# One pool of PSUM banks for the MLP and the segments, additions by VectorE in the last quarter, and memory rows turned earlier

## The chip, the core and the metric

The kernel runs on one core of a Trainium2 chip. The core has TensorE (matrix products, which it writes into PSUM), VectorE and ScalarE (elementwise work, both can read and write PSUM), GpSimd (POOL in the profile) and a queue engine, SP. DMA transfers between the DRAM and the on-chip memory SBUF are issued from SP, ScalarE or POOL, in each one's program order, and all of them run on the same 16 DMA engines. PSUM has eight banks; a bank holds 128 x 512 numbers of 32 bits, the result of one matmul of 512 columns. The metric is the device time of one execution in microseconds, as the median of several.

## The reference

The input x has 2048 tokens of 1024 numbers. It is normalized to xn, and two branches are added to it:

```python
x + A_ref(layernorm(x), mem0, Wq, Wk, Wv, Wo, 32) + B_ref(layernorm(x), w1, b1, w2, b2)

# B: an MLP over all tokens
h = gelu(xn @ w1 + b1)            # 2048 x 3584
return h @ w2 + b2                # 2048 x 1024

# A: 64 segments of 32 tokens, one after the other
mem = mem0                        # 8 rows of 1024
for s in range(64):
    h = concat([mem, xn[32*s : 32*s+32]])
    q, k, v = h @ Wq, h @ Wk, h @ Wv      # 32 heads of 128
    o = softmax(mask(q @ k.T / sqrt(128))) @ v
    o = o @ Wo
    mem = o[:8]                   # the next segment needs this
    outs.append(o[8:])
```

The segments depend on each other through the eight memory rows, while the MLP is free of such a chain. Data are bfloat16, sums are 32 bits.

## The kernel before

The work has two stages. First comes the MLP, in four quarters of 512 tokens. Then come the 64 segments. The code writes out the order of instructions by hand; each engine executes its own list in that order and waits on semaphores for the others.

A quarter of the MLP has 28 blocks of *first products* (`first_product`, L498): block fb takes 8 matmuls into one PSUM bank. ScalarE adds the bias (L572), VectorE and ScalarE compute GELU in several steps, and `gelu_tail` (L560, L561) writes the result, one of 28 blocks, into tiles called gT. Then come the *second products* of the quarter: for each of four groups of 128 tokens (t) and each half of the 1024 output columns (nb), 28 matmuls (fc = 0 to 27) are summed in one bank. In the first three quarters one bank after the other is completed (L619), VectorE adds the bias b2 (kept as the broadcast tile `b2bc`) and x, and the row is stored to the DRAM tensor `R_n` by `keep_R` (L448). `turn_R` (L485, L487) copies these rows into the layout in which the segments read them.

The last quarter (tg = 3) is different, because the memory of w1, w2 and gT is handed over to the weights of the segments while it runs. Of 64 weight units of 0.5 MB that a segment uses, 47 stay resident in SBUF (`fetch_resident`, L247 and L249) and 17 are streamed through six slots (`start_stream`, L279), two of these from copies kept in PSUM. A unit can be fetched as soon as the tile at its place has been read for the last time. During the last first products, every second block frees a tile of w1. Then, in the kernel before:

- `put_mem` (L315, L321, L325) turns the eight rows of mem0 with small matmuls against an identity into a bank of its own; VectorE copies them to `hr_home`, the operand of segment 0. After it, half of a unit of Wo is loaded over the source of these rows, into `d_oL` (L640).
- Eight banks are taken, six from the rotation of the first products (`ps`) and two from those used for transposes (`pT`); t = 3 has the latter two.
- For fc = 0 to 19 (`FC - TAIL`, TAIL = 8), each fc goes to all eight banks (L647), and `freed(fc)` then fetches the units that take the places of w2 and gT.
- For t = 3, the bias b2 and x are added by four matmuls: ones times the row b2 (L667) and identity times x (L669).
- For t = 0, 1, 2 the last eight fc are done one t after the other, and VectorE adds b2bc (L677) and x (L678).
- For t = 3 the last eight fc follow for each half; at the second half, `freed(20)` to `freed(27)` are called. The halves are copied out by ScalarE (L686), VectorE (L687) and ScalarE (L688), and `keep_R` issues the store from ScalarE's queue.

Only then does the pool of PSUM banks for the MLP end, and that of the segments begin: three banks that rotate as accumulators (`acc`), one for scores and other small things (`mixed`), and four that hold copies of weights (`kept`). Segment 0 begins with VectorE copying the preloaded halves of Wo from `d_oL` and `kq` into `kept` (L268), and TensorE starts the products for K (L791, from `half_pass`). They need the resident and streamed K units, `hr_home` with the memory rows, and a bank `acc`. In each segment the passes K, Q, K, Q, V, V of eight units each are followed by 16 units of Wo (L1049), and by `put_mem` for the next segment. Segment 0 also does the products for the last rows of four segments (`hrL`), and its pace of `unit_done` starts the following streams, seven late resident units and, in the following segments, the last rows of `turn_R` on POOL's queue.

The functions that the change touches, with their lines:

Of the kernel before, what the change touches and what calls it, by code (L numbers as in the profile page):

```python
# [10 lines left out]
BF16 = mybir.dt.bfloat16  # L11
# [6 lines left out]
P = 128  # L18
# [30 lines left out]
SCRATCH = 320  # L49
SMALL = 3776  # L50
LEAD = 6
TAIL = 8
EARLY_SEGS = 7
LEAD_FIRST = 4
SCORES_0 = (6, 6, 6, 5)
# [60 lines left out]
def kernel(  # L116
# [212 lines left out]


    NT = S // P
    with tc.tile_pool(name="ma", bufs=2) as ma, tc.tile_pool(name="mps", bufs=6, space=PSUM) as mps:
        eps_t = ma.tile([P, 1], F32, name="eps_t", bufs=1)
        nc.vector.memset(eps_t[:], EPS)
        ones = ma.tile([1, P], BF16, name="ones", bufs=1)
# [72 lines left out]
            return xn  # L408

        def turned(xn):  # L410
            pT = mps.tile([P, KT, P], BF16, name="pT", bufs=2)
            for kt in range(KT):
                nc.tensor.transpose(pT[:, kt, :], xn[:, kt * P:(kt + 1) * P], ident)
            return pT
# [88 lines left out]
                    stop=(kt == KT - 1),  # L503
                )

        def new_ps():
            return mps.tile([P, 512], F32, name="ps")

        idle = new_ps()
        for _ in range(WARM):  # L510
            nc.tensor.matmul(
# [24 lines left out]
        keep_xT(0, xnT)  # L536

        b1col = ma.tile([P, FC], F32, name="b1col", bufs=1)
        pst = mps.tile([P, KT, P], BF16, name="pT", bufs=2)
# [5 lines left out]
        for tg in range(4):  # L545
# [18 lines left out]
            for fb in range(FC):  # L564
                if tg == 0 and fb < len(begun):
                    ps = begun[fb]
                    first_product(ps, fb, xnT, 8, 16)
                else:
                    ps = new_ps()
                    first_product(ps, fb, xnT, 0, 16)  # L570
                xb = ma.tile([P, 512], BF16, name="g_xb", bufs=3)
                nc.scalar.activation(  # L572
                    out=xb[:, :], in_=ps[:, :], func=ACT.Identity, bias=b1col[:, fb:fb + 1], scale=1.0
                )
                u = ma.tile([P, 512], BF16, name="g_u")
                nc.vector.tensor_tensor(out=u[:, :], in0=xb[:, :], in1=xb[:, :], op=ALU.mult)
                nc.vector.tensor_scalar(
                    out=u[:, :], in0=u[:, :], scalar1=0.044715, scalar2=1.0, op0=ALU.mult, op1=ALU.add
                )
                nc.vector.tensor_tensor(out=u[:, :], in0=u[:, :], in1=xb[:, :], op=ALU.mult)  # L580
                if pend is not None:
                    gelu_tail(*pend)
                pend = (fb, u, xb)
                if last and fb % 2:
                    place = f"w1_{fb // 2}"
                    if place in RING:
                        start_stream(place)
                    else:
                        fetch_resident(place)
            gelu_tail(*pend)  # L590

            if tg == 0:
                for nb in range(2):
                    cs = slice(nb * 512, nb * 512 + 512)
                    ps = mps.tile([P, 512], F32, name="ps")
                    nc.tensor.matmul(ps[:, :], lhsT=ones[0:1, :], rhs=b2row[0:1, cs], start=True, stop=True)
                    nc.scalar.copy(out=b2bc[:, cs], in_=ps[:, :])

            if not last:
# [11 lines left out]
                for t in range(4):  # L611
                    ttg = 4 * tg + t
                    xn = ln_apply(ttg + 4)
                    rsb = xtoks[ttg]
                    for nb in range(2):
                        cs = slice(nb * 512, (nb + 1) * 512)
                        ps = mps.tile([P, 512], F32, name="ps")
# [12 lines left out]
                    keep_R(ttg, rsb)  # L630
# [3 lines left out]
            else:  # L634
# [6 lines left out]
                pss = [mps.tile([P, 512], F32, name="ps") for _ in range(6)]  # L641
                pss += [mps.tile([P, 512], F32, name="pT", bufs=2) for _ in range(2)]
                halves_of = [slice(512 * nb, 512 * nb + 512) for nb in range(2)]
                x = xtoks[4 * tg + 3]

                def second_product(fc, t, nb, stop):
                    nc.tensor.matmul(  # L647
                        pss[2 * t + nb][:, :],
                        lhsT=gts[fc // 4][:, fc % 4, t * P:(t + 1) * P],
                        rhs=w2_sb[fc // 2][:, fc % 2, halves_of[nb]],  # L650
                        start=(fc == 0),
                        stop=stop,
                    )

                def freed(fc):
                    if fc % 2:
                        fetch_resident(f"w2_{fc // 2}")
                    if fc % 4 == 3:
                        fetch_resident(f"gT{fc // 4}")

                for fc in range(FC - TAIL):
                    for t in range(4):
                        for nb in range(2):
                            second_product(fc, t, nb, False)
                    freed(fc)
                for nb, cs in enumerate(halves_of):
                    nc.tensor.matmul(pss[6 + nb][:, :], lhsT=ones[0:1, :], rhs=b2row[0:1, cs], start=False, stop=False)  # L667
                for nb, cs in enumerate(halves_of):
                    nc.tensor.matmul(pss[6 + nb][:, :], lhsT=ident, rhs=x[:, cs], start=False, stop=False)  # L669
                for t in range(3):  # L670
                    for fc in range(FC - TAIL, FC):
                        for nb in range(2):
                            second_product(fc, t, nb, fc == FC - 1)
                    r = xtoks[4 * tg + t]
                    for nb, cs in enumerate(halves_of):
                        ps = pss[2 * t + nb]
                        nc.vector.tensor_tensor(out=ps[:, :], in0=ps[:, :], in1=b2bc[:, cs], op=ALU.add)  # L677
                        nc.vector.tensor_tensor(out=r[:, cs], in0=ps[:, :], in1=r[:, cs], op=ALU.add)  # L678
                    keep_R(4 * tg + t, r)
                for nb in range(2):  # L680
                    for fc in range(FC - TAIL, FC):
                        second_product(fc, 3, nb, fc == FC - 1)
                        if nb:
                            freed(fc)
                    if nb == 0:
                        nc.scalar.copy(out=x[:, 0:512], in_=pss[6][:, :])  # L686
                nc.vector.tensor_copy(out=x[:, 512:768], in_=pss[7][:, 0:256])  # L687
                nc.scalar.copy(out=x[:, 768:1024], in_=pss[7][:, 256:512])  # L688
                keep_R(4 * tg + 3, x)

    with tc.tile_pool(name="late", bufs=1) as late, \
            tc.tile_pool(name="banks", bufs=1, space=PSUM) as banks:
# [15 lines left out]
        def let_go(ps):  # L713
            free_banks.append(bank_of.pop(id(ps))[0])

        mixed = banks.tile([P, 512], F32, name="mixed")
# [5 lines left out]
        masks_at = there[:, 32 * NL:32 * NL + NX + GRP * 16]  # L722
        mask_order = masks_at[:, 0:NX]
        mask_left = masks_at[:, NX:].rearrange("p (g q) -> p g q", g=GRP)
        kept = banks.tile([P, 4, 512], F32, name="kept")

        def keep(unit, c0, w, bank):

            copy_bits(kept[:, bank, :].bitcast(U32), w.bitcast(U32))
            kept_in.setdefault(unit, []).append((c0, kept[:, bank, :]))  # L730

        place_in_stream = {}

# [544 lines left out]
```

## Time and profile before

| | us |
|---|---|
| timed runs | 1809.34, 1813.58, 1815.01 |
| median | 1813.58 |
| profiled execution, its own time | 1810.81 |
| its span, first to last instruction | 1809.0 |
| first products of the last quarter begin | 311.7 |
| second products of the last quarter begin | 360.3 |
| segment 0 begins | 414.7 |
| memory rows for segment 1 (L315) | 452.5 |
| memory rows for segment 2 | 475.8 |
| TensorE busy, of the span | 1702.7 (94%) |
| VectorE / ScalarE / GpSimd busy | 983.8 / 686.6 / 300.5 |

Times within the span count from its first instruction. In the profile's rows, PE is TensorE, PEld its loading of the stationary operand, DVE is VectorE, ACT ScalarE; SPq and ACTq are issues of DMA transfers from these queues. "L791" is line 791 of the kernel. A row of the list of waits reads "who waits <- for whom: us in total, times, longest". In the table by stretches each row has the stretch, its length, the busy time of TensorE, its loads, VectorE, ScalarE and GpSimd with the number of instructions, the granted TensorE clock as a share of full speed, the share of the DMA engines' time in use, and GB/s. In the chain, each row is a start, a duration and the work that held the end at that point.

### The profile page before, as it was taken

Reading aid. Unit: us, or ns where it says so; the run is one execution under the profiler, and the core shown is the slowest. Engines: PE = TensorE matmul, PEld = TensorE weight load, DVE = VectorE, ACT = ScalarE, POOL = GpSimd, SP = SyncE. Lnnn points to the kernel's source line nnn. Section 1 sums busy time; section 2 is a strip of 40 time slices with the busy share of each in tenths; the row PEclk is TensorE's granted clock in tenths of the full one; section 3 lists DMA queues with packets and bytes.
Section 4 is the critical chain, followed back from the end, with each engine's and each line's share of the span. In section 5 each row is a group of like instructions: output and inputs, shape, how many; then the busy total and the mean of one; then the engine's idle time right before and its main releaser. Section 6 shows DMA issues by size and latency. Waiting matters only on the chain.

```text
span 1809.0 us, 71476 instructions
## 1 busy us (share of the span) xinstructions
PE 1702.7 (94%) x31161; PEld 894.6 (49%) x31161; DVE 983.8 (54%) x2517; ACT 686.6 (38%) x1698; POOL 300.5 (17%) x586
## 2 busy tenths in 40 slices
PE   8999999997999999999999999999999999999998
PEld 4444444444445555555554555554545555555544
DVE  7657483805555555555555555555555555555544
ACT  6334260702333333333333334343433334334333
POOL 0000000411132111111111212111111211111111
PEclk9999999999999999999999999999999999999999
DMA  9931111769999999999999999999999999999998
GB/s 289 310 100 48 53 48 37 247 221 339 370 385 389 376 385 374 386 374 379 387 380 380 385 396 388 384 389 364 382 384 375 387 369 393 380 375 392 384 390 315
DMA packets 221310, 592.07 MB, mean 327 GB/s; under 512 B 46195, under 2 KB 76515, under 8 KB 220996
## 3 DMA queue, kind: packets, MB, share of 16 engines
q1 hardware_dynamic: 197584, 567.08, 83.7%
q0 software_dynamic: 16896, 16.85, 2.9%
q8 instruction: 244, 4.00, 0.9%
q10 hardware_dynamic: 6516, 3.57, 0.7%
q14 instruction: 70, 0.57, 0.1%
HBM read 573.43 MB, written 28.90 MB: 333 GB/s over the span
## 4 chain that ended last, share of the span: by engine, by line
PE 78%; DMA 11%; DVE 4%; ACT 4%; issue 3%; ACTq 0%; DVEq 0%; POOL 0%; POOLq 0%
PE acc L791 38%; PE acc L1049 12%; PE ps L498 11%; PE ps L619 8%; DMA u<-Wc_O 7%; DMA u<-Wc_V 3%; PE ps L647 2%; ACT mixed L960 2%; PE acc L1000 1%; PE mixed L908 1%; DVE kq L875 1%; DVE pd_main L973 1%; ACT kq L870 1%; PE pT L647 1%; PE mixed L914 1%
## 5 line engine op out<-in xcount | busy, mean ns | idle before, releaser
L791 PE MATMUL acc<-u,hr_home 128*32 128x512 bf16 x11520 | 760.2, 380 | 16.7 <-issue 7.3
L791 PEld LDWEIGHTS <-hr_home 128*32 128x32 bf16 x12288 | 351.0, 96 | 286.0 <-issue 39.1
L791 PE MATMUL acc<-u,hrL 128*32 128x512 bf16 x2880 | 256.4, 380 | 6.4 <-issue 3.8
L498 PE MATMUL ps<-u 128*128 128x512 bf16 (+1 forms) x920 | 194.4, 374 | 2.0 <-ACT u L418 2.0
L268 DVE TENSOR_SCALAR u<-kept 128x512 uint32<-128x512 uint32 x254 | 163.2, 684 | 57.9 <-PE acc L791 43.4
L843 ACT CAST d_oL<-acc 128x512 bf16<-128x512 f32 x143 | 82.0, 584 | 263.3 <-PE acc L791 254.8
L619 PE MATMUL ps<-u 128*128 128x512 bf16 x672 | 147.0, 379 | 0.0
L1049 PE MATMUL acc<-u,d_oL 128*32 128x512 bf16 x1944 | 132.7, 381 | 9.7 <-issue 6.0
L498 PEld LDWEIGHTS <-u 128*128 128x128 bf16 x920 | 89.8, 98 | 104.9 <-issue 2.4
L1049 PEld LDWEIGHTS <-kq 128*32 128x32 bf16 x3908 | 102.7, 96 | 76.5 <-ACT kq L1019 21.8
L973 DVE TENSOR_TENSOR pd_main<-kq,mixed 128x320 bf16<-128x320 bf16 x128 | 62.5, 488 | 133.1 <-ACT mixed L960 133.1
L875 DVE STREAM_TRANSPOSE kq<-kq 128x512 bf16<-128x512 bf16 x128 | 91.1, 711 | 73.5 <-ACT kq L870 71.1
L870 ACT CAST kq<-acc 128x512 bf16<-128x512 f32 (+2 forms) x192 | 85.3, 444 | 114.5 <-PE acc L791 84.8
L1049 PE MATMUL acc<-u,kq 128*32 128x256 bf16 (+1 forms) x2372 | 116.0, 313 | 13.6 <-DMA u<-Wc_O 11.4
L1240 POOL DMA_DIRECT2D out_dram<-hr_home x168 | 85.2, 514 | 221.5 <-DVE hr_home L1207 221.1
L847 ACT CAST kq<-acc 128x512 bf16<-128x512 f32 x128 | 75.1, 587 | 111.6 <-PE mixed L914 105.5
L791 PEld LDWEIGHTS <-hrL 128*32 128x32 bf16 x3072 | 88.1, 96 | 59.0 <-issue 6.0
L938 DVE TENSOR_TENSOR kq<-kq,mixed 128x96 bf16<-128x96 bf16 (+1 forms) x256 | 38.1, 190 | 125.5 <-ACT kq L928 68.6
L619 PEld LDWEIGHTS <-u 128*128 128x128 bf16 x672 | 65.3, 98 | 77.4 <-DVE g_u L580 0.4
L1049 PEld LDWEIGHTS <-d_oL 128*32 128x32 bf16 x2592 | 65.3, 96 | 66.1 <-issue 20.0
L572 ACT ACTIVATE g_xb<-ps,b1col 128x512 bf16<-128x512 f32 x112 | 76.8, 686 | 55.5 <-PE ps L498 54.7
L960 ACT ACTIVATE mixed<-mixed,small_consts 128x160 f32<-128x160 f32 x256 | 94.2, 368 | 8.4
(133 smaller groups left out, 2010.4 us busy)
## 6 DMA issues: line engine op xcount, KB each, us to landing
u<-Wc_K SPq DMA_DIRECT2D x256, 512.0 KB
u<-Wc_V SPq DMA_DIRECT2D x256, 512.0 KB
u<-Wc_O SPq DMA_DIRECT2D x256, 512.0 KB
u<-Wc_Q SPq DMA_DIRECT2D x192, 512.0 KB
u<-in_B_w_dram SPq DMA_DIRECT2D x28, 512.0 KB
u<-in_A_Wq_dram SPq DMA_DIRECT2D x13, 512.0 KB
u<-in_A_Wv_dram SPq DMA_DIRECT2D x12, 512.0 KB
u<-in_A_Wk_dram SPq DMA_DIRECT2D x9, 512.0 KB
```

The lines of the kernel that those rows point to most:

```text
L268: nc.vector.tensor_single_scalar(out=out, in_=in_, scalar=0, op=ALU.bitwise_or)
L498: nc.tensor.matmul(ps[:, SEG * s0:SEG * s1].rearrange("p (s t) -> p s t", t=SEG), lhsT=w1_sb[fb // 2][:, kt, (fb % 2) * P:(fb % 2 + 1) * P ...
L572: nc.scalar.activation(out=xb[:, :], in_=ps[:, :], func=ACT.Identity, bias=b1col[:, fb:fb + 1], scale=1.0)
L619: nc.tensor.matmul(ps[:, :], lhsT=gts[fc // 4][:, fc % 4, t * P:(t + 1) * P], rhs=w2_sb[fc // 2][:, fc % 2, cs], start=(fc == 0), stop=(fc ...
L791: nc.tensor.matmul(o, lhsT=lhs[:, i, :], rhs=m, start=(i == seq[0]), stop=(i == seq[-1]), tile_position=(0, 32 * j),)
L843: cp(out=out, in_=ps.rearrange("p (h e) -> p h e", e=32))
L870: nc.scalar.copy(out=q_home[:, h0:h1, NL:40], in_=ps[:, 32 * h0:32 * h1].rearrange("p (h e) -> p h e", e=32))
L875: nc.vector.transpose(out=home, in_=home)
L960: nc.scalar.activation(out=mixed[:, 160 * b:160 * b + 160], in_=mixed[:, 0:160], func=ACT.Exp, scale=-1.0, bias=off[:, b:b + 1],)
L973: nc.vector.tensor_tensor(out=pdA.rearrange("p c b q -> p b c q"), in0=prA[:, None, :, :].to_broadcast([P, 2, 4, 40]), in1=dd, op=ALU.mult,)
L1049: nc.tensor.matmul(acc[r0:r0 + rows, 0:256 * len(blocks)], lhsT=lhsT, skip_group_check=True, rhs=o_columns(t, k, blocks), start=start, sto ...
L1240: loads.dma_start(out=out_flat[rows, 256 * j:256 * j + 256], in_=res[32 * j:32 * j + NX, :])
```

## The change

One pool of eight PSUM banks, with one tag per bank, now serves both stages. `new_ps` hands out banks 0 to 5 in turn for the products, 6 and 7 for transposes. The accumulators of the segments get the banks of the last quarter's t = 0 and the first half of t = 1, `mixed` the second half of t = 1, and `kept` (now four tiles instead of one) those of t = 2 and t = 3. So each user of a bank waits for the bank's last user alone.

`put_mem` and the load into `d_oL` move to block 20 of the last quarter's first products; `put_mem` takes one bank from the rotation there.

In the second products of the last quarter, t = 0 runs two steps (AHEAD) ahead of the others, and all eight banks go through all 28 fc without a separate tail. The four matmuls for b2 and x are gone. Instead VectorE adds b2bc and x into each bank in the middle of its sum: bank n after fc = 3 + 2n. The matmul of that bank for the next fc is left out at its step, and made up one step later, just before the regular one. A unit is fetched when all eight banks have used the tile at its place. At the end the banks are only copied out: t = 0 by VectorE and ScalarE when it is complete, 12 matmuls before the last; then t = 1 and t = 2 by both, and t = 3 by ScalarE alone.

```diff
-TAIL = 8
+AHEAD = 2
+ADD_FIRST = 4
+ADD_STEP = 2
+MEM_AT = 20
...
+    banks = ctx.enter_context(tc.tile_pool(name="banks", bufs=1, space=PSUM))
+    turns = {"ps": deque(range(6)), "pT": deque((6, 7))}
+    def new_ps(way="ps"):
+        k = turns[way][0]
+        turns[way].rotate(-1)
+        shape, kind = ([P, 512], F32) if way == "ps" else ([P, KT, P], BF16)
+        ps = banks.tile(shape, kind, name=way, tag=f"bank{k}")
+        place_of[id(ps)] = k, ps
+        return ps
...
+                if last and fb == MEM_AT:
+                    put_mem(o_sb, nxt["hT"], new_ps(), wide=False)
+                    nc.sync.dma_start(out=d_oL[:, 0:DM], in_=Wo_v[:, h + 1, :])
...
-                put_mem(o_sb, nxt["hT"], mps.tile([P, 512], F32, name="ps"), wide=False)
-                nc.sync.dma_start(out=d_oL[:, 0:DM], in_=Wo_v[:, h + 1, :])
...
+                    taken[fc] += 1
+                    if taken[fc] == 8:
+                        if fc % 2:
+                            fetch_resident(f"w2_{fc // 2}")
+                        if fc % 4 == 3:
+                            fetch_resident(f"gT{fc // 4}")
+
+                def row_out(t, engines):
+                    x = xtoks[4 * tg + t]
+                    for nb, cp in enumerate(engines):
+                        cp(out=x[:, 512 * nb:512 * nb + 512], in_=pss[2 * t + nb][:, :])
+                    keep_R(4 * tg + t, x)
...
-                for nb, cs in enumerate(halves_of):
-                    nc.tensor.matmul(pss[6 + nb][:, :], lhsT=ones[0:1, :], rhs=b2row[0:1, cs], start=False, stop=False)
-                for nb, cs in enumerate(halves_of):
-                    nc.tensor.matmul(pss[6 + nb][:, :], lhsT=ident, rhs=x[:, cs], start=False, stop=False)
...
+                add_at = {ADD_FIRST + ADD_STEP * n: n for n in range(8)}
+                for step in range(FC + AHEAD):
                     for t in range(4):
+                        fc = step if t == 0 else step - AHEAD
+                        if not 0 <= fc < FC:
+                            continue
                         for nb in range(2):
...
+                            n = 2 * t + nb
+                            if add_at.get(fc) == n:
+                                continue
+                            if add_at.get(fc - 1) == n:
+                                second_product(fc - 1, t, nb)
+                            second_product(fc, t, nb)
+                            if add_at.get(fc + 1) == n:
+                                ps, cs = pss[n], slice(512 * nb, 512 * nb + 512)
+                                for r in (b2bc, xtoks[4 * tg + t]):
+                                    nc.vector.tensor_tensor(out=ps[:, :], in0=ps[:, :], in1=r[:, cs], op=ALU.add)
+                    if step == FC - 1:
+                        row_out(0, (nc.vector.tensor_copy, nc.scalar.copy))
+                for t, engines in ((1, (nc.scalar.copy, nc.vector.tensor_copy)), (2, (nc.scalar.copy, nc.vector.tensor_copy)), (3, (nc.scalar.copy, nc.scalar.copy))):
+                    row_out(t, engines)
...
-        free_banks = deque(f"acc{k}" for k in range(3))
+        free_banks = deque(f"bank{k}" for k in seg_banks[:3])
...
-        kept = banks.tile([P, 4, 512], F32, name="kept")
+        kept = [banks.tile([P, 512], F32, name="kept", tag=f"bank{k}") for k in seg_banks[4:]]
```

More of the change, by code (lines that the diff above doesn't have):

```diff
@@ L331 @@
     NT = S // P
-    with tc.tile_pool(name="ma", bufs=2) as ma, tc.tile_pool(name="mps", bufs=6, space=PSUM) as mps:
+    banks = ctx.enter_context(tc.tile_pool(name="banks", bufs=1, space=PSUM))
+    turns = {"ps": deque(range(6)), "pT": deque((6, 7))}
+    place_of = {}
+    def new_ps(way="ps"):
[5 more added lines that the diff above has]
+        return ps
+    with tc.tile_pool(name="ma", bufs=2) as ma:
         eps_t = ma.tile([P, 1], F32, name="eps_t", bufs=1)
@@ L410, in turned @@
         def turned(xn):
-            pT = mps.tile([P, KT, P], BF16, name="pT", bufs=2)
+            pT = new_ps("pT")
             for kt in range(KT):
@@ L504, in first_product @@
                 )
-        def new_ps():
-            return mps.tile([P, 512], F32, name="ps")
         idle = new_ps()
@@ L538 @@
         b1col = ma.tile([P, FC], F32, name="b1col", bufs=1)
-        pst = mps.tile([P, KT, P], BF16, name="pT", bufs=2)
+        pst = new_ps("pT")
         pst_flat = pst.rearrange("p a b -> p (a b)")
@@ L594 @@
                     cs = slice(nb * 512, nb * 512 + 512)
-                    ps = mps.tile([P, 512], F32, name="ps")
+                    ps = new_ps()
                     nc.tensor.matmul(ps[:, :], lhsT=ones[0:1, :], rhs=b2row[0:1, cs], start=True, stop=True)
@@ L616 @@
                         cs = slice(nb * 512, (nb + 1) * 512)
-                        ps = mps.tile([P, 512], F32, name="ps")
+                        ps = new_ps()
                         for fc in range(FC):
@@ L638, with second_product @@
                 start_stream("xn3")
-                put_mem(o_sb, nxt["hT"], mps.tile([P, 512], F32, name="ps"), wide=False)
-                nc.sync.dma_start(out=d_oL[:, 0:DM], in_=Wo_v[:, h + 1, :])
[L641 to L646, printed above, removed]
+                pss = [new_ps() for _ in range(6)]
+                pss += [banks.tile([P, 512], F32, name="ps", tag=f"bank{k}") for k in turns["pT"]]
+                seg_banks = [place_of[id(ps)][0] for ps in pss[:6]] + list(turns["pT"])
+                taken = [0] * FC
+                def second_product(fc, t, nb):
                     nc.tensor.matmul(
@@ L649, in second_product @@
                         lhsT=gts[fc // 4][:, fc % 4, t * P:(t + 1) * P],
-                        rhs=w2_sb[fc // 2][:, fc % 2, halves_of[nb]],
+                        rhs=w2_sb[fc // 2][:, fc % 2, nb * 512:nb * 512 + 512],
                         start=(fc == 0),
-                        stop=stop,
-                    )
[L655 to L659, printed above, removed]
@@ L661 @@
-                for fc in range(FC - TAIL):
+                        stop=(fc == FC - 1),
+                        skip_group_check=True,
+                    )
+                    taken[fc] += 1
[9 more added lines that the diff above has]
+                    keep_R(4 * tg + t, x)
@@ L668 @@
-                for nb, cs in enumerate(halves_of):
[L669 to L689, printed above, removed]
@@ L696 @@
-    with tc.tile_pool(name="late", bufs=1) as late, \
-            tc.tile_pool(name="banks", bufs=1, space=PSUM) as banks:
+                            n = 2 * t + nb
[8 more added lines that the diff above has]
+                                    nc.vector.tensor_tensor(out=ps[:, :], in0=ps[:, :], in1=r[:, cs], op=ALU.add)
@@ L698 @@
+                    if step == FC - 1:
+                        row_out(0, (nc.vector.tensor_copy, nc.scalar.copy))
+                for t, engines in ((1, (nc.scalar.copy, nc.vector.tensor_copy)), (2, (nc.scalar.copy, nc.vector.tensor_copy)), (3, (nc.scalar.copy, nc.scalar.copy))):
+                    row_out(t, engines)
+    with tc.tile_pool(name="late", bufs=1) as late:
         nc.scalar.preload_act_table_set("natural_log_exp_and_others")
         small = deque()
-        free_banks = deque(f"acc{k}" for k in range(3))
+        free_banks = deque(f"bank{k}" for k in seg_banks[:3])
@@ L714, in let_go @@
             free_banks.append(bank_of.pop(id(ps))[0])
-        mixed = banks.tile([P, 512], F32, name="mixed")
+        mixed = banks.tile([P, 512], F32, name="mixed", tag=f"bank{seg_banks[3]}")
         trs = [
@@ L724 @@
         mask_left = masks_at[:, NX:].rearrange("p (g q) -> p g q", g=GRP)
-        kept = banks.tile([P, 4, 512], F32, name="kept")
+        kept = [banks.tile([P, 512], F32, name="kept", tag=f"bank{k}") for k in seg_banks[4:]]
         def keep(unit, c0, w, bank):
-            copy_bits(kept[:, bank, :].bitcast(U32), w.bitcast(U32))
-            kept_in.setdefault(unit, []).append((c0, kept[:, bank, :]))
+            copy_bits(kept[bank].bitcast(U32), w.bitcast(U32))
+            kept_in.setdefault(unit, []).append((c0, kept[bank]))
         place_in_stream = {}
```

2 lines of the change are left out of this document (removed).

## The prediction, made before the run

> **What bounds the kernel now.** I read five views, from the whole to the place of the edit. The first is the page: shares of the chain that ended last, and the row of DMA traffic over 40 slices of 45.2 us.
>
> ```profile
> PE 78%; DMA 11%; DVE 4%; ACT 4%; issue 3%; ACTq 0%; DVEq 0%; POOL 0%; POOLq 0%
> GB/s 289 310 100 48 53 48 37 247 221 339 370 385 389 376 385 374 386 374 379 387 380 380 385 396 388 384 389 364 382 384 375 387 369 393 380 375 392 384 390 315
> ```
>
> TensorE carries 78% of the chain. The weights stream at about 385 GB/s from slice 10 on, but only 221 and 339 GB/s pass in slices 8 and 9 (362 to 452 us), where the last quarter of the MLP meets segment 0. All edits lie between the first products of that quarter (from 311.7 us) and segment 0. The second view is the chain in order of time there.
>
> ```profile
> 363.32 0.23 DVE hr_home L325
> 363.60 0.38 PE ps L647
> 363.97 0.43 PE pT L647 x2
> 364.40 2.33 PE ps L647 x6
> 366.73 0.85 PE pT L647 x2
> 367.59 1.52 PE ps L647 x6
> 369.11 0.43 PE pT L647 x2
> ...
> 398.90 0.53 PE pT L667 x2
> 399.43 0.54 PE pT L669 x2
> 399.97 10.36 PE ps L647 x48
> 410.33 3.47 PE pT L647 x16
> 413.82 0.43 DVE u L687
> 414.28 0.38 ACT u L688
> 414.70 5.17 PE acc L791 x92
> 419.87 11.12 DMA u<-Wc_Q
> ```
>
> The chain leaves TensorE at three points: for VectorE's copy of the memory rows (L325), for the copies that end the MLP (L687, L688), and in segment 0 for weights. Matmuls of 512 columns come every 0.216 us (48 in 10.36 us). The third view is TensorE's list of waits from 360 to 480 us: total, times, longest.
>
> ```profile
> PE acc L791 <- DMA u<-Wc_Q: 2.8, 2, 1.7
> PE ps L647 <- DVE hr_home L325: 2.0, 1, 2.0
> PE acc L791 <- DMA u<-Wc_V: 1.8, 4, 0.9
> PE acc L1049 <- DMA u<-Wc_O: 1.7, 3, 0.7
> PE acc L791 <- ACT u L688: 0.9, 1, 0.9
> PE acc L791 <- DMA hrL<-rowsL_d: 0.8, 1, 0.8
> ```
>
> The fourth is the table by stretches: after the 2.0 us wait the granted clock (third column from the right) was 0.63 and 0.52 for two stretches of 2 us; and from 404 to 406 us the DMA engines moved nothing.
>
> ```profile
> 364.00:366.00 2.00, 2.00 (x7) 0.75 (x6) 0.00 (x0) 0.00 (x0) 0.00 (x0) 0.63 0.80 215
> 366.00:368.00 2.00, 2.00 (x6) 0.76 (x5) 0.00 (x0) 0.00 (x0) 1.05 (x2) 0.52 0.94 375
> 404.00:406.00 2.00, 2.00 (x11) 0.88 (x10) 1.96 (x3) 0.00 (x0) 0.00 (x0) 1.00 0.00 0
> ```
>
> The fifth, the instructions on the tile ps, prices the additions (ns: least, median, most).
>
> ```profile
> L677 DVE TENSOR_TENSOR ps<-ps,b2bc x6: 689/694/700, 403.2 to 411.5; 128x512 f32<-128x512 f32 x6
> L678 DVE TENSOR_TENSOR u<-ps,u x6: 691/692/692, 404.0 to 412.2; 128x512 bf16<-128x512 f32 x6
> ```
>
> **The change, part by part.**
>
> *Memory rows amid the first products (put_mem at block 20).* The eight small matmuls (0.23 us together at 360.15) and VectorE's copy (0.22 us) are moved, not removed. What goes is the wait: the sixth bank of the second products was put_mem's own, and its copy stood behind the last GELU steps in VectorE's queue, until 363.6. In the new place the bank is asked for again six blocks later, 6 x 8 x 0.216 = 10.4 us, and the copy is queued behind two to three GELU steps of 0.4 us. Gain: 2.03 us.
>
> The half clock goes with it: the 17 matmuls from 363.60 to 369.11 took 5.51 us against 17 x 0.216 = 3.67. Gain: 1.84, say 1.85 us. What shows that the wait caused it: idles of 1.68 us (before 428.4) and 1.77 us (before 435.0) left the clock at 1.00 in this trace, that of 2.03 did not. Ends: 0 (it was not the wait) and 1.85; I take 1.85.
>
> [...]
>
> The copy of Wo's half into d_oL moves ahead of four w1 fetches, xn2 and xn3 on SP's queue. It waits only for put_mem's matmuls, and the fetch behind it for the next block anyway. Cost 0; without that cover one block, 1.7 us, on a queue with idle DMA engines behind it.
>
> *Bias and x by VectorE.* Four matmuls go (L667, L669): 0.53 + 0.54 = 1.07 us. There come 16 additions in place of 12; each pair takes 1.43 us (403.24 to 404.67). A bank's matmul is left out at one step and made up at the next, so between two uses of it lie 14 other matmuls, 3.0 us, less 0.2 us of the last one's tail: 2.8 us of cover for 1.43 us plus a handover. VectorE is idle there otherwise (the stretches from 364 on show 0.00). The tightest is the first, behind the last GELU product, which ends at 363.4; bank 0 is left at about 363.3 and wanted at about 366.1. Cost 0; if the cover went, 8 x 1.43 = 11.4 us.
>
> *Row 0 two steps ahead, banks handed on one by one.* Segment 0's first product takes the bank of row 0, emptied some 18 matmuls (3.9 us) before the end; before, it waited 413.80 to 414.70 for L687 and L688. Gain 0.90 us. The banks at the start of the second products have slack too: row 0 goes alone for two steps, and the bank of block 27 is wanted nine matmuls (1.9 us) on, its reading by ScalarE over after 0.7.
>
> ScalarE now holds four of the last six evacuations and three stores behind the last matmuls: copies 0.59, a store's issue 0.33 (rows 413.39 and 414.68), then the table load 1.28. Counted through, its last copy ends 2.4 us and the table load 4.0 us after the last matmul; before, the table load ended 1.6 us after segment 0's start. The first K evacuation queued behind it ends at about 4.8 us, before at 3.4 (417.52 + 0.58 - 414.70); its bank is wanted by the second accumulator of Q at 4.3 (419.01). VectorE's keep copies wait for row 3 and come 1 to 1.5 us later too; the scores that need them start 10 us in. Cost 0.5 us, ends 0 and 1.4.
>
> *Weights earlier.* Before, six fetches of 0.52 MB (w2_10 to w2_13, gT5, gT6) were all released by the last eight matmuls: at segment 0's start 3.15 MB were outstanding, 7.9 us at the 400 GB/s of the stretches 420 to 450. Now a row is released once all banks took it: 44, 28, 12 and 0 matmuls before the end, that is 9.5, 6.0 (two), 2.6 and 0 us (two). At 1.31 us each and some 2 us of landing, about 2.5 of them (3.3 us) are left at the start. The lead is 4.6 us. Against it: row 12's rows on POOL's queue, issued from 408.75 (6 us ahead of the start), now come at the start; 14 small transfers, at most 0.8 us. The waits for weights and rows to 470 us sum to 2.8 + 1.8 + 1.7 + 0.8 = 7.1 us. DMA engines are full from 416 to 452, so a lead shortens these waits one for one until they are gone: 3.8 us; I take 3.5, since a 1.8 us wait for VectorE's qL lies amid them. Ends: -0.8 and 7.1.
>
> From segment 1 on every engine's order is the same as before; the phase from 480 us (TensorE waits 16.1 us for weights in 1,329 us) is only shifted.
>
> **Sum.** 2.03 + 1.85 + 1.07 + 0.90 - 0.5 + 3.5 = 8.85 us. The profiled execution took 1810.81 (span 1809.0 and 1.8 around it): 1801.96. The timed runs were 1809.34, 1813.58 and 1815.01, the median 2.8 above the profiled one. I take the mean of the four, 1812.2, as the level: 1803.3, rounded to 1803.
>
> **The rivals.**
>
> *A. TensorE's gain alone.* Segment 0 gets no faster, as the DMA engines set its pace whatever was fetched ahead. For: they are full from 416 to 452 us. Against: some four transfers fewer are queued at its start. Gain 5.85 - 0.5 = 5.35: 1806.8.
>
> [...]
>
> *C. The segments give it back.* They run at 385 GB/s against 400 at best, close to what the engines can do; a start at another phase of ScalarE's and POOL's loads could stretch each period by 0.15 us, 61 times 9 us. Against: only 16.1 us of waiting for weights in 1,329. Time: 1812.
>
> *D, the other side. The additions block TensorE.* If a pair's result came later than the 2.8 us of cover, each of eight banks idles TensorE; where such an idle reaches 2 us it also costs the 1.85 us of half clock. For: each pair sits in the middle of a bank's chain. Against: 1.3 us of slack. The gain is used up at 1.1 us per bank; with a full 2.0 + 1.85 each, 31 us less 8.85: 1834. It decides from 1.8 us per bank on (0.3% slower).
>
> **How the numbers follow.** Forecast 0.58, A 0.13, B 0.08, C 0.12, D 0.09. A measurement of this kernel can tell 0.3%, 5.4 us: faster is below 1808.1, slower above 1819.0. Faster: 0.58 + 0.08 + most of A (0.11) = 0.77. Same: C and the rest of A = 0.14. Slower: D = 0.09. The low end: all 7.1 us gained and no cost on ScalarE, 12.95 from 1810.81, is 1797.9; 1797 with the scatter. The high end takes in A, B and the better part of C: 1811. Left out: part of C, and D.
>
> **What would show it.** In the profile after: no wait of L660's matmuls (the second products there) for hr_home and a clock of 1.00 throughout 360 to 370; no matmuls from b2row; 224 second products in about 48.4 us; the first segment product right behind the last of them, near 408.8; 16 additions of 0.70 us between 363 and 400 with no wait for them on TensorE; traffic above 200 GB/s from 398 to 410; the Wc_Q waits of segment 0 gone or under 1 us; put_mem of segment 1 (L315 at 452.5) near 443.7. The forecast is wrong if TensorE waits for VectorE amid the second products, if the evacuations behind ScalarE hold up Q by over 1.4 us, or if segment 0 still takes 37.8 us from its first product to that put_mem.

## The result, and the profile after

The changed kernel took 1800.54 us (median of nine runs, 1797.04 to 1806.8), the kernel before 1813.58 us (nine runs). The ratio is 0.9938, with a 95% interval from 0.9918 to 0.9958, that is 7.6 to 14.9 us faster. In a later comparison it was 0.9963 (0.9945 to 0.9982), or 3.3 to 10.0 us. The forecast was 1803 us, 8.85 us faster, and that gain lies in both. Single runs of one kernel scatter by 10 us and more, so the parts are read from landmarks inside the profiles below, not from totals.

The profiled execution after has a span of 1798.2 us, 10.8 less. First the chain in order of time, at the three places where it left TensorE before:

```profile
348.58 0.15 PE ps L324 x8
348.74 12.19 PE ps L513 x56
360.93 0.43 PE ps L660 x2
...
404.58 3.85 PE ps L660 x17
408.43 0.02 issue
408.45 0.70 DVE u L678
```

Memory rows are turned at 348.6 amid the first products (L513), without a break before the second products (L660). The chain of this profile leaves TensorE at 408.4, but TensorE itself goes straight on: in its timeline the first product of segment 0 starts at 409.20, while the last second product, begun at 408.9, is still ending. TensorE's list of waits from 300 to 480 us:

```profile
PE acc L797 <- DVE qL L849: 2.0, 2, 1.8
PE acc L1055 <- DMA u<-Wc_O: 1.5, 2, 0.8
PE mixed L914 <- DVE kq L881: 1.1, 3, 0.5
...
PE acc L797 <- ACT d_oL L849: 0.5, 1, 0.5
PE acc L797 <- DMA u<-Wc_V: 0.5, 1, 0.5
```

The waits for hr_home (2.0 us), for L688 (0.9) and for Wc_Q (2.8) are gone, and no second product waits for an addition. New is the 0.5 us for a bank that ScalarE empties late. The table by stretches, with the granted clock third from the right:

```profile
364.00:366.00 2.00, 2.00 (x11) 0.94 (x10) 1.39 (x3) 0.00 (x0) 0.34 (x1) 1.00 0.96 350
366.00:368.00 2.00, 2.00 (x11) 0.93 (x10) 0.56 (x1) 0.00 (x0) 0.00 (x0) 1.00 0.98 365
404.00:408.00 4.00, 3.95 (x19) 1.79 (x19) 0.69 (x1) 0.59 (x1) 0.00 (x0) 1.00 0.91 308
437.08:440.49 3.41, 1.50 (x32) 0.79 (x32) 2.31 (x6) 0.49 (x2) 0.00 (x0) 1.00 1.03 406
440.49:443.90 3.41, 3.41 (x64) 2.92 (x60) 1.18 (x4) 0.74 (x2) 0.00 (x0) 0.50 1.05 400
```

Between 364 and 368 us the clock is full where it was half in the profile before. From 404 to 408, shortly ahead of segment 0, 308 GB/s pass; in the profile before, the stretches of 2 us from 404 to 414 had 0, 131, 0, 172 and 72 GB/s. But half clock now stands inside segment 0, from 440.49 to 443.90 us. The instructions on the tile ps give the additions at the expected price:

```profile
L697 DVE TENSOR_TENSOR ps<-ps,b2bc x8: 691/700/700, 364.0 to 392.9; 128x512 f32<-128x512 f32 x8
L697 DVE TENSOR_TENSOR ps<-ps,u x8: 699/700/700, 364.7 to 393.6; 128x512 f32<-128x512 f32 x8
```

The landmarks of all profiles, in us, are read from TensorE's timeline. "Second products" runs from their first to the first product of segment 0. "Segment 0" runs from there to the memory rows for segment 1, "segment 1" on to those for segment 2, and "the rest" from there to those for segment 63.

| kernel | second products | segment 0 | segment 1 | sum of the three | the rest |
|---|---|---|---|---|---|
| before | 54.39 | 37.70 | 23.33 | 115.42 | 1307.6 |
| before, again | 52.67 | 37.80 | 22.97 | 113.44 | 1320.0 |
| before, a third time | 52.69 | 37.86 | 22.93 | 113.48 | 1314.4 |
| changed | 48.44 | 35.48 | 21.71 | 105.63 | 1306.1 |
| changed, again | 48.44 | 35.61 | 22.22 | 106.27 | 1309.4 |
| put_mem moved alone | 50.50 | 37.61 | 23.56 | 111.67 | 1308.0 |
| fetches held in the code only | 48.44 | 35.60 | 21.83 | 105.87 | 1303.3 |
| fetches truly held | 48.44 | 40.05 | 24.05 | 112.54 | 1310.6 |
| six additions a bank | 61.42 | 35.98 | 22.34 | 119.74 | 1315.1 |
| last banks first | 51.19 | 34.57 | 22.90 | 108.66 | 1312.1 |
| table load early | 48.44 | 34.71 | 22.48 | 105.63 | 1307.1 |
| late units early | 48.44 | 32.37 | 22.38 | 103.19 | 1303.1 |
| both of these | 48.44 | 31.50 | 23.63 | 103.57 | 1310.6 |

The first three columns repeat within some tenths of a us for one kernel, except where the clock differs. The rest scatters by 12 us among three profiles of one kernel, which is why the total says so little.

### The profile page after: what moved, and what is told of

The parts are those of the page before. It is cut to its first block, busy times and chain, and to the rows that moved or that the text cites. A ratio compares the mean times of both kernels' runs of the same rounds, so it can differ in the third digit from the quotient of the medians.

```text
span 1798.2 us, 71469 instructions
## 1 busy us (share of the span) xinstructions
PE 1705.1 (95%) x31137; PEld 894.2 (50%) x31157; DVE 988.9 (55%) x2523; ACT 689.2 (38%) x1701; POOL 301.7 (17%) x586
## 4 chain that ended last, share of the span: by engine, by line
PE 77%; DMA 10%; ACT 4%; DVE 4%; issue 3%; ACTq 0%; POOL 0%; DVEq 0%; POOLq 0%; SPq 0%
PE acc L797 37%; PE acc L1055 13%; PE ps L513 11%; PE ps L634 8%; DMA u<-Wc_O 6%; DMA u<-Wc_V 3%; PE ps L660 3%; ACT mixed L966 2%; PE acc L1006 2%; DVE kq L881 1%; PE mixed L914 1%; DVE pd_main L979 1%; ACT kq L876 1%; DMA u<-Wc_K 1%; ACT mixed L963 1%
## 5 line engine op out<-in xcount | busy, mean ns | idle before, releaser
L513 PE MATMUL ps<-u 128*128 128x512 bf16 (+1 forms) x920 | 194.6, 373 | 2.0 <-ACT u L433 2.0
L513 PEld LDWEIGHTS <-u 128*128 128x128 bf16 x920 | 89.7, 98 | 104.7 <-issue 2.4
```

Of the source, the lines that this page charges most:

```text
L513: nc.tensor.matmul(ps[:, SEG * s0:SEG * s1].rearrange("p (s t) -> p s t", t=SEG), lhsT=w1_sb[fb // 2][:, kt, (fb % 2) * P:(fb % 2 + 1) * P ...
```

## The experiments

The experiments test the terms of the forecast one by one, and with them the rivals: A (early weights bring nothing), B (the slow clock has another cause), C (the segments give the gain back) and D (the additions block TensorE).

**The memory rows alone.** In the kernel before, with its own pools, put_mem and the load behind it move to block 20.

```diff
-                put_mem(o_sb, nxt["hT"], mps.tile([P, 512], F32, name="ps"), wide=False)
-                nc.sync.dma_start(out=d_oL[:, 0:DM], in_=Wo_v[:, h + 1, :])
...
+                if last and fb == 20:
+                    put_mem(o_sb, nxt["hT"], new_ps(), wide=False)
+                    nc.sync.dma_start(out=d_oL[:, 0:DM], in_=Wo_v[:, h + 1, :])
```

> The kernel before, with put_mem and the load into d_oL moved to block 20 and nothing else. Before, the stretch from the first second product to the first product of segment 0 took 54.39 us (360.31 to 414.70). If the 2.03 us wait also caused the slow clock behind it (my reading): 54.39 - 2.03 - 1.85 = 50.5 us, clock 1.00 throughout 360 to 370. If the slow clock has another cause (rival B): 52.4 us, with a stretch near half clock left. Segment 0, from its first product to the memory rows of segment 1, stays at 37.8 us in both cases.

Measured: 50.50 us, segment 0 unchanged with 37.61. Its table by stretches:

```profile
362.00:366.00 4.00, 4.00 (x20) 1.85 (x19) 1.51 (x5) 0.73 (x2) 1.65 (x3) 1.00 0.90 306
366.00:370.00 4.00, 4.00 (x21) 1.79 (x19) 0.00 (x0) 0.00 (x0) 1.64 (x4) 1.00 0.83 317
```

TensorE is busy throughout, at full clock. This agrees with my number, but does not yet show that the wait caused the slow clock: for that one has to see what the clock does when the wait is there.

**The kernel before, twice more.**

> The kernel before once more: 54.4 us from the first second product to segment 0, with the 2.03 us wait. If that wait causes the slow clock each time, the clock falls again between 364 and 368 us. [...]

> The same again: 54.4 us with the slow clock, or 52.5 us without.

Both have the 2.0 us wait for hr_home, and both took 52.7 us instead of 54.4 (54.39 less the 1.85 us of my term is 52.5): the clock stayed at 1.00 behind the wait. What differs is seen from where the slow clock begins. Wherever half clock comes in the 13 profiles before the end of TensorE's work, it lasts 3.41 us (6.83 twice, in one profile), and within one profile such pieces begin whole multiples of 3.413 us apart: in the changed kernel's at 440.49, 570.19 and 976.38, which are 38 and 119 such steps apart. Steps of 3.413 us, laid through a profile from such a piece, are called its grid here; the position differs from profile to profile. Here are rows cut along the grid, first of the profile before, then of the first of the two further ones:

```profile
361.10:364.51 3.41, 1.38 (x8) 0.54 (x6) 1.95 (x6) 0.99 (x2) 1.66 (x3) 1.00 0.79 191
364.51:367.92 3.41, 3.41 (x10) 1.22 (x9) 0.00 (x0) 0.00 (x0) 0.97 (x2) 0.50 0.90 324
```

```profile
359.63:363.05 3.42, 2.79 (x20) 1.11 (x19) 2.93 (x9) 2.17 (x4) 1.60 (x4) 1.00 0.59 205
363.05:366.46 3.41, 2.04 (x10) 0.97 (x10) 0.90 (x4) 0.63 (x1) 0.92 (x2) 1.00 0.71 228
366.46:369.87 3.41, 3.41 (x18) 1.52 (x17) 0.00 (x0) 0.00 (x0) 1.75 (x4) 1.00 0.95 335
```

In the first execution the wait (361.57 to 363.60) lies whole in one stretch of the grid. TensorE is busy for 0.40 of it, and the next stretch has half clock. In the second execution a border at 363.05 cuts the wait (362.42 to 364.42) in two, TensorE is busy for 0.82 and 0.60, and no half clock follows; in the third a border at 363.78 cuts it likewise. The count over all profiles goes with this. The clock fell 25 times in them, each time behind a grid stretch in which TensorE was busy for 0.23 to 0.56 of the time. Of the grid stretches at full clock, all ten with less than 0.42 were followed by half clock, 15 of the 70 from 0.42 to 0.56, and none of the 6,743 busier ones. What tells the 15 from the other 55 is not shown.

So half clock came behind the wait in the one execution whose grid did not cut it. By these lengths a wait of 2.03 us lies whole in a stretch of 3.41 us in (3.41 - 2.03) / 3.41 = 0.40 of all positions of the grid, as an estimate; it was one execution of three. The half clock costs 54.39 - 52.68 = 1.71 us when it comes, about 0.7 on average by that estimate. What moving put_mem saves each time is 52.68 - 50.50 = 2.2 us.

**Longer and shorter idles.** Six additions per bank in place of two, by taking b2 off and adding it again:

```diff
-                                for r in (b2bc, xtoks[4 * tg + t]):
+                                b, x = b2bc, xtoks[4 * tg + t]
+                                for r, op in ((b, ALU.add), (b, ALU.subtract), (b, ALU.add), (b, ALU.subtract), (b, ALU.add), (x, ALU.add)):
```

> The changed kernel with six additions per bank in place of two (b2 added, taken off, added, taken off, added, then x). The six take 6 x 0.72 = 4.3 us against a cover of 2.8, so TensorE should wait some 1.5 us for VectorE at each of eight banks: second products to segment 0 48.4 + 12 = 60.4 us. Each wait is shorter than 1.77 us, which left the clock at 1.00 before the change: if the clock goes by a single idle, it stays at 1.00 here. If it goes by the busy share over some microseconds (eight waits, one in every 5 us, busy share 0.7), it falls, and 8 x 1.85 = 15 us more are lost. If the cover is smaller than I counted (rival D), the waits are 2 us and more.

Its list of waits from 360 to 423 us has one row, and of its table by stretches two are shown:

```profile
PE ps L660 <- DVE ps L698: 11.7, 8, 1.6
```

```profile
366.00:370.00 4.00, 2.35 (x12) 1.00 (x11) 2.97 (x5) 0.00 (x0) 1.33 (x3) 1.00 0.63 242
370.00:374.00 4.00, 2.57 (x13) 1.11 (x12) 3.50 (x5) 0.00 (x0) 2.53 (x5) 1.00 0.60 199
```

The second products took 61.42 us, 13.0 more than in the changed kernel, of which 11.7 are these waits: eight of 1.5 us on average, as worked out. So the cover is 4.3 - 1.5 = 2.8 us, and the changed kernel's pair of 1.4 us has 1.4 us to spare. The clock stayed at 1.00 although TensorE was busy only 59 to 64% of these stretches; along this profile's grid (its position read from the one fall, behind the end of the work), no stretch of the second products was busy for less than 0.52.

Reversed banks, so that segment 0 starts with the banks that are emptied last:

```diff
-                seg_banks = [place_of[id(ps)][0] for ps in pss[:6]] + list(turns["pT"])
+                seg_banks = ([place_of[id(ps)][0] for ps in pss[:6]] + list(turns["pT"]))[::-1]
```

> The changed kernel with the banks given to the segments in reverse: the accumulators of segment 0 are those that ScalarE empties last, 2.7 us after segment 0 could begin (411.9 against 409.2). If the choice of banks is what closed the gap of 0.90 us: TensorE waits 2.7 us ahead of segment 0 here, second products to segment 0 51.1 us, and an idle of that length should halve the clock for about 4 us, which costs some 1.8 us in segment 0 unless weights are late anyway. If one pool in place of two is enough by itself: 48.4 us.

TensorE waited 2.7 us for L678, and the second products took 51.19 us: it is the choice of banks that closes the gap, not the one pool by itself. (What row 0's lead of two steps adds to the choice was not tried alone.) The clock did not do what I expected. The table by stretches of this kernel, along its grid:

```profile
407.12:410.53 3.41, 2.44 (x12) 0.97 (x10) 1.80 (x4) 1.04 (x2) 0.04 (x1) 1.00 0.88 321
410.53:413.94 3.41, 1.70 (x32) 0.95 (x35) 1.54 (x5) 2.49 (x4) 1.61 (x3) 1.00 0.96 237
413.94:417.36 3.42, 3.42 (x68) 1.92 (x64) 1.65 (x3) 0.59 (x1) 0.00 (x0) 1.00 1.03 370
441.25:444.66 3.41, 1.55 (x52) 1.07 (x40) 1.46 (x4) 0.63 (x2) 0.00 (x0) 1.00 1.04 393
444.66:448.07 3.41, 3.09 (x30) 1.03 (x34) 0.42 (x2) 0.00 (x0) 0.00 (x0) 0.50 0.98 389
```

The idle of 2.7 us (409.56 to 412.24) was cut at 410.53, TensorE was busy for 0.72 and 0.50 of the two stretches, and the clock stayed at 1.00. Later in the same profile a wait of 2.1 us for rows (hrL), whole in the stretch from 441.25, was followed by half clock. In the changed kernel's three profiles single waits of at most 0.9 us were enough, close together in one stretch that was busy for 0.39 to 0.53 (the first of them in the row from 437.08 above). So in these profiles no length of a single idle tells the falls from the rest; the busy share of a grid stretch does, outside 0.42 to 0.56.

**The weights.** First I held the six fetches of fc 20 to 27 in the code until the last second products.

```diff
-                    if taken[fc] == 8:
-                        if fc % 2:
-                            fetch_resident(f"w2_{fc // 2}")
-                        if fc % 4 == 3:
-                            fetch_resident(f"gT{fc // 4}")
+                    if taken[fc] == 8:
+                        for f in range(20, FC) if fc == FC - 1 else [fc] if fc < 20 else []:
+                            if f % 2:
+                                fetch_resident(f"w2_{f // 2}")
+                            if f % 4 == 3:
+                                fetch_resident(f"gT{f // 4}")
```

> The changed kernel, with the six fetches of fc 20 to 27 (w2_10 to w2_13, gT5, gT6) held until the last second products, as before the change. Second products to segment 0: 48.4 us as in the changed kernel. If the early fetches pay for what segment 0 gained: it takes 35.6 us in the changed kernel, here 37.8 to 39.4 (2.2 us gained there, up to the 3.8 that I worked out for the lead), with waits for Wc_Q back. If the DMA engines set the pace whatever is fetched ahead (rival A): 35.6 us.

It held nothing: SP's issues are at the same distances from segment 0 as in the changed kernel (the four fetches of Wo from 5.52 us ahead of it in both). Where a transfer stands among TensorE's instructions in the code changed nothing here, with the order in SP's queue and its waits as they were. It serves as a third profile of the changed kernel: 35.60 and 21.83 us.

To hold them, the tiles must be in use. So bank 7 does its last eight matmuls at the very end:

```diff
-                            if add_at.get(fc) == n:
+                            if add_at.get(fc) == n or (n == 7 and fc >= 20):
                                 continue
...
+                for fc in range(20, FC):
+                    second_product(fc, 3, 1)
```

> The changed kernel with the last eight matmuls of bank 7 (fc 20 to 27) done at the very end, so that the six tiles are in fact read to the end, as before the change; nothing else is moved. (In the run with held fetches the SP queue came out the same as in the changed kernel, since only the order within the queue counts, so it held nothing.) Second products to segment 0: 48.4 us. If the early fetches pay for what segments 0 and 1 gained (35.5 and 21.7 us against 37.7 and 23.3 before): 37.7 and 23.3 us here, and waits for Wc_Q of 2 to 3 us back. If the DMA engines set the pace whatever is fetched ahead (rival A): 35.6 and 22 us.

Segments 0 and 1 took 40.05 and 24.05 us, 6.3 to 6.9 us more than in the changed kernel's three profiles (57.2 to 57.8), and the waits for weights are back. TensorE's list of waits from 355 to 480 us:

```profile
PE acc L799 <- DMA u<-Wc_Q: 5.0, 2, 3.7
PE acc L799 <- DMA u<-Wc_V: 2.9, 3, 2.0
PE acc L799 <- DVE qL L851: 1.8, 1, 1.8
PE acc L1057 <- DMA u<-Wc_O: 1.7, 3, 0.7
PE acc L799 <- DMA hrL<-rowsL_d: 0.7, 1, 0.7
```

Rival A is refuted: without the early fetches, segments 0 and 1 lose all that they had gained, and more. The hold even costs more than before the change (64.1 against 60.8 to 61.0 us). Two likely reasons, not separated here, are that segment 0 begins 0.9 us sooner after the last matmul, and that SP itself was held up; of SP's waits from 403 to 445 us:

```profile
SPq L282 <- DMA u<-Wc_V: 3.3, 2, 2.3
...
SPq L250 <- DMA R_n<-u: 3.0, 2, 2.5
SPq L282 <- DMA u<-in_A_Wv_dram: 2.5, 1, 2.5
```

A streamed unit (L282) waited 2.5 us for a fetch from the weights' source tensor to land, and the first one was issued 6.0 us into segment 0 (at 414.90, segment 0 from 408.88) instead of 2.2 in the changed kernel and 3.0 in the kernel before.

**Fetching still earlier.** If segment 0 is short of DMA time, its seven late units are the next load to move. Five of them need the memory of the GELU tiles, which is free when the second products begin:

```diff
+                ma_scope.close()
+                late = ctx.enter_context(tc.tile_pool(name="late", bufs=1))
+                for unit in LATE:
+                    t = late.tile([P, 2048], BF16, name="W_" + "_".join(map(str, unit)))[:, :]
+                    res_tiles[unit] = t
+                    fetch(t, unit)
...
-        b2bc = ma.tile([P, DM], BF16, name="b2bc", bufs=1)
+        b2h = [vl.tile([P, 512], BF16, name=f"VL{nb}") for nb in range(2)]
```

> The changed kernel with the five late resident units of Wo (2.6 MB) fetched at the start of the second products, where 230 GB/s pass, in place of segment 0; the memory of the GELU tiles is handed on there, and b2 is kept in the later VL tiles. If segment 0 is bound by the DMA engines: their load there falls by 2.6 MB, 6.5 us at 400 GB/s; the waits for weights left in the changed kernel (0.5 + 1.5 us and the 1.8 us of slow clock behind them) go: segment 0 32 us in place of 35.6, and segment 1 up to 1 us faster; total 3 to 5 us faster than the changed kernel. If segment 0 is bound by its own chain of dependent steps: 35 us, no change.

Segment 0 took 32.37 us, 3.1 to 3.2 less than the changed kernel, without half clock; segment 1 did not gain (22.38). The list of waits of this kernel from 355 to 475 us:

```profile
PE acc L801 <- DVE qL L853: 2.0, 2, 1.8
PE acc L1010 <- DVE VL L857: 0.6, 1, 0.6
PE acc L801 <- DMA u<-Wc_V: 0.6, 1, 0.6
PE acc L801 <- DMA hrL<-rowsL_d: 0.6, 1, 0.6
PE acc L801 <- ACT d_oL L853: 0.5, 1, 0.5
```

The waits for Wc_O are gone; what is left are mostly the segment's own steps. The three landmarks together gain 2.4 to 3.1 us, less than the 3 to 5 expected. Part of this is the half clock in segment 0, which the changed kernel's three profiles have and this one does not; the fairer pair is the next experiment's, both without it, where the late units gain 105.63 - 103.57 = 2.1 us. The total was 0.9947 of the kernel before (0.9925 to 0.997), beside 0.9963 (0.9945 to 0.9982) for the changed kernel in the same comparison: the intervals overlap, so the totals do not show the gain.

> The changed kernel once more, for comparison on the same chip: 0.994 of the kernel before.

**The table load.** The load of ScalarE's table moves to the start of the second products, alone and together with the late units:

```diff
                 start_stream("xn3")
+                nc.scalar.preload_act_table_set("natural_log_exp_and_others")
...
-        nc.scalar.preload_act_table_set("natural_log_exp_and_others")
```

> The changed kernel with the load of ScalarE's table (1.28 us) moved from behind the last stores to the start of the second products, where ScalarE is idle. In the changed kernel TensorE waits 0.52 us in Q's pass of segment 0 for an accumulator that ScalarE empties late (my cost of 0.5 us), and 0.19 us for qL. If the table load is what makes it late, both waits go: 0.5 to 0.7 us, if weights are not late there next. No change to be measured in the total.

> The early late units and the early table load together: 3.5 to 5.5 us faster than the changed kernel if both readings hold, 0.991 of the kernel before; no gain over the changed kernel if segment 0 is bound by its own steps.

The 0.5 us wait for ScalarE is gone from the list of waits. The landmarks' sum is 105.63 as without it, although no half clock fell in segment 0 here: waits for Wc_O rise to 2.3 us, so weights are late next. The ratios to the kernel before are 0.9966 (0.9944 to 0.9987), and with both 0.9935 (0.9911 to 0.996). Against the changed kernel, none of the three is resolved by its total.

## Why the prediction was right or wrong

*The wait for the memory rows, 2.03 us: right.* Moving put_mem alone shortened the stretch by 2.2 us against the two executions before at full clock.

*The half clock behind it, 1.85 us: right in that it came with the wait, wrong as a sure gain.* The step that failed is "Ends: 0 (it was not the wait) and 1.85; I take 1.85", together with the proof ahead of it: the lengths of three idles in one trace cannot show whether the clock falls each time. The same wait was followed by the slow clock in one of three executions, where it lay whole in one stretch of the grid, and a 2.7 us idle elsewhere, cut by the grid, was followed by none. The execution whose profile I used was the one with it, so I counted a chance event in full. The changed kernel has such an event itself: in all three of its profiles the clock fell around 440 us, for one stretch of 3.41 us, which at a clock of 0.50 costs at most half of that, 1.7 us. This agrees with the position of the grid too. The grids of the three happen to lie within 0.6 us of each other there (stretches from 437.08, 437.17 and 436.62), and five variants with other grids or another course of segment 0 had full clock throughout it (true hold, six additions, table load early, late units, both). In "table load early" the same waits for Wc_O were spread over stretches that were busy for 0.84 and 0.51, and no half clock followed. In these profiles the clock thus gave no sure gain.

Rival B, that the slow clock has another cause and stays, expected 52.4 us from put_mem alone; that took 50.50, at a clock of 1.00 from 362 to 370 us. It was right in so far as the wait does not tell by itself: with the same wait, the clock fell in one execution and stayed at 1.00 in two, with other positions of the grid.

*The four matmuls and the gap, 1.07 + 0.90 = 1.97 us: right.* From put_mem alone to the whole change the stretch falls from 50.50 to 48.44, by 2.06 us. That the gap goes by the order of the banks is shown by the reversed order, which brings 2.7 us back.

*The additions at no cost: right.* No second product waits for VectorE, and the six additions show the cover to be 2.8 us. Rival D needs a chain on VectorE longer than that: three times the additions brought it, with 11.7 us of waiting. (Its limit of 1.8 us per bank counts from the level of 1812.2 us; by the stated limit of 1819.0 it is 2.0.)

*ScalarE's late evacuations, 0.5 us: right in the profile* (0.52 us, gone with the early table load), though without effect on the sum, as weights are late next.

*Earlier weights, 3.5 us: right, by and large.* Segments 0 and 1 together take 57.2 to 57.8 us against 60.8 to 61.0, 2.9 to 3.8 less, with the 0.5 us on ScalarE and a half clock in segment 0 already paid. That the cause is the earlier fetches is shown by the true hold, and by the late units, which gain more by fetching still earlier. How much the fetches are worth is not shown by the hold: its cost of 6.3 to 6.9 us exceeds the gain, as held fetches also delay the streams behind them in SP's queue, which I had not counted.

*The rest only shifted: neither shown nor refuted.* In the pair of profiles the lead of the changed kernel is 7.7 us at the memory rows for segment 1, 9.3 for segment 2, about 5 around segment 30 and 10.8 at the end. Three profiles of the kernel before differ by 12 us there, and half clock is a part of this: it lasted 0, 13.7 and 6.8 us there, which costs at most 0, 6.8 and 3.4 us. Rival C's 9 us of stretching would have shown (1306.1, 1309.4 and 1303.3 against 1307.6, 1320.0 and 1314.4), a change of 2 or 3 us would not.

In sum, at full clock before, the landmarks give 113.46 - 105.9 = 7.5 us, with the half clock in the changed kernel's segment 0 still in it, against 5.85 - 1.85 + 3.0 = 7.0 by my terms without the clock. The forecast of 8.85 was right in its direction and nearly so in size, with one term of luck in it. The medians of the timed runs differ by 13.0 us in the first comparison and by 7.0 in the later one, which had more runs; what the first has beyond these parts is not explained.

## What to carry to other kernels

Where one stage hands PSUM over to the next, give the next stage's first accumulators the banks that are emptied first, and let each bank be waited for alone. Where a stage is short of DMA time at its start, what counts is when the tiles that its fetches overwrite are read for the last time: change the order of the reads. Fetches moved in the code alone left SP's issues where they were (5.52 us ahead of segment 0), and segment 0 at 35.60 us; tiles read to the end made it 40.05. Price a slow clock from several executions, never from one: here it followed the same wait in one of three.

## What the runs showed of the hardware that I had not expected

Half clock came in pieces of 3.41 us (twice of 6.83). In one profile they began whole multiples of 3.413 us apart (38 and 119 steps in the changed kernel's, 440.49 to 976.38 us), at positions that differed between executions. Each of the 25 falls in 13 profiles stood behind a grid stretch in which TensorE was busy for 0.23 to 0.56 of the time. So the same 2.0 us wait was followed by half clock in one of three executions of one kernel, at a cost of 1.71 us; a cut idle of 2.7 us and eight waits of 1.5 us were not followed by it, while waits of at most 0.9 us close together were.
